# A stored instruction order replaced by another one: same operations, other PSUM banks, other casting engines

## Chip, core and metric

One core of one Trainium2 chip runs the kernel. The metric is the device time of one execution in microseconds (us), from the first to the last thing that the device does for it; the span in a profile runs from the first to the last instruction and is a few us shorter. The core has five engines that each work through a queue of their own in order: TensorE (PE in the profile; its weight loads are the row PEld), VectorE (DVE), ScalarE (ACT), GpSimd (POOL) and SyncE (SP), which here does nothing but issue transfers. Matrix products land in PSUM, eight banks of 128 partitions x 512 float32; VectorE or ScalarE must read them out before a bank can be used again.

## The reference

Two independent layers on bf16 inputs, 2048 tokens by 640 channels each, side by side in the output.

```python
# A: short causal filter of k, product with v, long causal convolution, gate
k_shift = sum over t of k_pad[:, t:t + S, :] * shift_k[:, ks - 1 - t]     # ks = 4
kv = k_shift * v
y = irfft(rfft(kv, 2S) * rfft(ssm_k, 2S))[:S] + kv * ssm_D
a = q * y
# B: 32 heads of 20, 4 segments of 512 tokens, a running memory M, z
for s in range(4):
    p = softmax(qs @ ks.T * scale + causal_mask)
    a_dot = p @ vs
    a_mem = (phi(qs) @ M) / (phi(qs) @ z + 1e-6)
    outs.append(g * a_mem + (1 - g) * a_dot)          # g = sigmoid(beta)
    M, z = M + phi(ks).T @ vs, z + phi(ks).sum(0)
b = concat(outs) @ wo
return concat([a, b], axis=-1)
```

## The kernel before

The program is first recorded and then issued. Python code calls the engines through a `Recorder`; each call, or each run of matmuls into one PSUM group, becomes one of 1505 operations, and each PSUM region that an operation fills becomes one of 471 groups. Nothing is sent to the chip until the end, when `rec.issue(order, base)` goes through the list `order` and issues the operations in that sequence; `base` says at which of the eight PSUM banks each group starts. Both lists are stored in the file as compressed text, `ORDER` and `BASE`. Every engine executes its own operations in the order in which they stand in `ORDER`, and waits only where an operation needs a result, or a buffer or bank that is still being read. All records have one line of the profile, L261, so operations are told apart by the tiles they read and write.

A third string, `EVICT`, has one digit for each of 227 casts that empty a PSUM bank into bf16: 1 puts the cast on VectorE, 0 on ScalarE (`evict`).

The operations, with the short names used below:

- `warm.n`: ten products of zeros at the start. `taps`: the four-tap filter, loaded as `load.skr` (tile `qabs`), turned by TensorE and cast to `taps`. `skd.d`: twenty small ScalarE products that build diagonal matrices of the taps for the five channel blocks d; those of d = 3, 4 read `pack`, a 117.5 KB table of constants loaded as `load.pack` by the GpSimd queue; the others read `ident`.
- Layer A, for each of five blocks d of 128 channels: `A.d.kt` or `ss` (the long filter, turned into tile `kT`), `FK` (its spectrum: eight groups of products with `Wf`, each cast into tile `F`), `BK` (butterflies on VectorE into `Kh`), `ks` (the short filter as products of `kr` with `skd`, multiplied by v on VectorE into `vt`), `FX` and `BX` (the same spectrum of `vt`), `P1` to `P3` and `YB` (complex product and butterflies on VectorE), `I` (inverse, multiplied by q on VectorE).
- Layer B, for eight units u (segment u // 2, half of the heads u % 2): `xt` (x turned into `xT`), `P.u.t` (k and q of token tile t, two groups, cast to `KQ`), `V.u.t` (v, cast to `Va`), `KT` (transposing DMA to `KQT`), `phi`, `kam`, `bound` and `rows` (a bound of each row's logits, written back by four DMAs), `mem` (the memory), `S.u.g.D`, `.A`, `.J` (logits of a head group; each is two ScalarE exponentials of 128x1024 into tile `ET`), `O` (products with v and with the memory), `N` (division on VectorE), and per segment `ot` and `W` (output projection; the last segment's comes at the very end).

The lists interleave the convolution blocks with the attention units, so that the exponentials of ScalarE and the butterflies of VectorE run at the same time, with TensorE feeding both.

```python
def evict(self, out, in_, grp):
    ...
    if EVICT[e] == "1":
        self.nc.vector.tensor_copy(out=out, in_=in_, grp=grp)
    else:
        self.nc.scalar.copy(out=out, in_=in_, grp=grp)
...
order, base = unpack(ORDER, len(rec.ops)), unpack(BASE, len(rec.groups))
with tc.manual_schedule():
    rec.issue(order, base)
```

Of the kernel before, what the change touches and what calls it, by code (L numbers as in the profile page):

```python
# [995 lines left out]
ORDER = r"""
c-jrtgMttW5Czb=Gk0=rwrjI(+um&3wry{=YqM?Jwr#$5zT#w+Y?57aNKVNmxh0R}l_(NXTtrGs6^SI}q@v`L>Jn9=NgOF7p(MXlmGV+nk_aWQR+7{bAQdE|RFeV{Sqe%KEhI&?uv8XEKCPs6rKXsuRMxIiTWU#W
Ni5MNro@oa8cWJ(eyt%v(p?H@LP;gXw2qY3G*Vw`YC~x*^`x9;k=D{uifcCs(gxB<+DZ!vEw!|<l$177TboKh=^^bTtyIx;Qc-(J9c?9bwU0EBdfH6VOM5A$9i^(ql_FAH3Tl6;p*^Lr_LjcVLCWhO=_CWBn8cG|
l3cpT2<a@brG(Vi1d>RGNJA|u4K%C_mN7C=hRY~PDPd%s43)7mTB>OyEupJ*yo{6yQb>b!gErRcx<}S%d?~3-wTaHry|PjlX$tA4$t076lL|UfR%vscB$H)|?2`~(tW#yPY?AI;N@mDL-7l?lnrzbPazK`751p$s
rL`{AHabt6X<PlJEwsHJm6qB;=W9EiC0pg7bkd&MOBZNIJtlp1wj7qux=jwrHr=jAq__6bwc16y>Kxgj+hv^|my6O*Pe`!r)M2_=FUeI|p$m1m_SY>sK(EPMiDM&lr^K~gx>YaBX_+VEb-rAYcy>mX%Pxs(6Lp|2  # L1000
kli{#<J%57FN1WCuGif%Mx$A38>fq8uP&6NwnZ+;GTo<R^{gzG!MaSA>p3~5`!%Jdv7tIdPs&n>k5rb-qT6vjpp$f(PS;a1QV(i)nXEDFzKqsUn%Ex7bD5$`WQNYv>oQeu$qKn4H|4e**2j{>?#L{CDR<?NX0{`m
!B)#reIT<n0UpU~c_nM)jjWVJc2QqQR768Uq_DTLN)jQXWwQ11L@wz&$zoUZvOblha!sE}R@)$JB{9-lcDt&lb)CGIVV1)_N-`uzY&)w@bhw?-50V5S@>DlUPCKE`^ppl7DRS8-IjK`@gq_o=Hqr)KbX?FBh#<H1
yymvg5(9ZHrp2<<_#$bM#|GIqiHSS<Q19wjNrUV9NMqr#-q4$x4!884=CeMCjkkJVze|35pg&~1^|v^9r|<QZCbzU!!0yQ}iHiZ26|XhWe##roh<JFeza^bzLT3Dx43f>p+8>!<FSMY&)C86dAM}g<laKmU$5=uO
g-@CVpS7fY(}_0DfYO#8-!(J@KeUu(fFV03SxV$U8B2wqTGkZPtgscbB38+!8&S?8ps4jjWgBJ1tcp1zA}2;$aVuf7E!YNIE_A{Wt7>5|%Vt;}6h}3yZecOgCR+*Au-qt$APa|@79Qm-5{hAt<;7g9VEIrUg;5rz
QPE0bp1ri%))xVoZ-G+BDxe(dS`jR?0jOuStPB=eJ1d3yRuBQ~U_&iG8rV8pZ0)VJ^+!WnZ(t!Tu`rCxwicUhOxeOJVyO*8SjJ%#4na$+gk`qeMxd2d!3vAYMm7kQF%-iv5-V+i4Mt;YYE8`eTZf}6R#`QWG1=V4
U>us+Sj6H6tAUL+9^n`n9j%jvXJ-qs1YB)vY^`;%C@@RNuJ%{E8LczA+g9sg|Fox7M=$Gb+pLd?ZMXRB&P42Mn=A<va|$+FKXZ#j*cR)CP!@xCFqFG3G?TI)doTinFpSB$$EKn`yJG_O+78=i1+d?0;(-0piHOKR
*2Y1L#va&ZJFN@i@{mPmEhOU^i^qHDz&^Z-!`2gZ(3L58&d%B;>&trR#*`d|RJ>xBZ5q<B7mnHt)W<P9V#n=-rDjLY#7V1*(Ku!2tv9Bl0WMlZYY68gq-AKkV4>I*H!K~S;-=lQ!3?nG7{c2Y+3uKHW8AgLxM%Hn
)goDYUbFjXg!IhJ>z0uN*pv5dEHiOAnxGj@+hWYZ1AAnT?THQIQ=5%B2xFr-kip2pUR;9VoQs9%#0;E=wFqmYxdJ1&2wC~edb2Yh+Ip<R7`8)pF2xf(w`^R7hse!w+<<3zfc6;Ayd24ie2Ud*fjnG^HCTm7e2yG!
gPhF8`MANB$j1c;L4HnV7q-F_w#6k}Mr%x^djW>>f}GAG6feZ0gim8(7Go6Kh#7og#aW4=eI{REGfJ>BH=zpuvLv^lBevotI-mx__&5Gz5P$GHtFk74avQ4gJxg-}w__H|uq?~*Bdhb3T|q6DVtIbx96rJhd}19|
U@))ZG3K&1>vA?Dcmp<MBhF(*?!+}T<~O`S6E<aie!(vMVLgVk>-dhhXvRg{jfNi4!`oMUwi{^97Hr8@T+Hykg!8!vk-Rl;;<bITM*h*%7jgk3`&Yh#`7N~JC+x#gwq<*#f3nwjhbSK8x3Qe-xEB#@89R7XU(cGp  # L1010
9~&6L6?~7+*vMn}fK{yJoA?o{xsnI4mSH`bH}i0Q5NmiGwLQAOvwdvt@9hWnv%VkTQT)Ua1b7VJ%q`r?ZQRZV9@7uwAY=I<9O7ZN^&Q;FuNK=|czoZ@Jv@QE{DseK=dN-5H;(Wx{@@D(^dwsPQ6A$dgwns3*#F_p
{}GDkyLcM^40?)@HHp8qq#oDLK((uzez4O#i{tF#)Dt|zvka>z+0D-}wAS-5dY(NziiX#4n!qD!R6U2D9zoCJ7ZZ6Tji$-`0u%ZV>*W{O*?%*-CikBf=$CkzSD3<6`EN_<S9y(ptc~aQ>x`+ry^mi+L2v3Yw6Ul5
0^ZNRSsG90!t|cOGkR=|rD^@UHSs*2*ZX=t&*c5Rm1p(=UdV5<h+n`XX7y~I-Q#Kw&*FtWr^nG>*4m5uV?N+*=JMiR!i)Js-r^v?!%{xPOM4kF>*YM2j`Nb9+XwmtkFR%G-k-375BBl?ibMS#6KW;D&(}<#!@aUs
@$O#HhxrJv>Q7n66KN8y<|BQSKjUamtj}53$9Q$`=t;GcPxRC})?aXnPxVRulGA*;FZap*hRJk>ukac^(--<m-|ve(xz6@rpW}1=Ef4q-Po=Ybk*CzXo>7;28lC6!eV?!O6q-|)`38T-OuF7fe4{V$O&+MZbd_)R
b-u+9`XNuN>2$T{(af4&*Z5Z7=2>;S@9=E8(|7r9&!C5Wk00@io<(!(ZNKD4J-Z(B9D2s@_+7u}_x-G&^YebeFZ&h0>eu|b-|(A$%a8jBKk29ZwEqW|<?eI
"""
BASE = r"""
c-mc30kQ=l2qH7P|Bb%^HT(YTw3QJeIRFd<sz+jRy?dN_c64=g_q;oTp3i@FZ1$>p9(|HVZ-8vexIrYy61*|F0uj5v$#^nzP{qkt%qZ3%W{_Dok{Dq(H71#r0akn%z}00Jclvx$gQ@^)TGSeh?zfxH6-23;AWyw`
GIDlB{xWvhS!ov&h=r?#|M|G__KO;hF6kM(S=4$QIhkND<bo948P26xGGo5nVNc4hxwzjS4d5wUc|FGXSBGkq=gZwN=<DsC!5i{ii1N6e#&bEJpTGK5VbBdR*N<D$R8}UvVRi9&tDtL19a6U4NyYE>db(@z-nc&e
zj<yB_0_Fy+ZU-_pF7vVd_53;{d!F5fS_B_eBS8~RvQK@  # L1020
"""


# [69 lines left out]
```

## Time and profile before

| | |
|---|---|
| time, three runs | 268.57, 269.68, 269.82 us; median 269.68 |
| profiled execution, span | 266.3 us |
| its own time beside the span | not recorded apart; the median run is 3.4 us over the span |
| PE busy | 257.8 us (97%), 4323 matmuls |
| ACT busy | 248.8 us (93%), 392 instructions |
| DVE busy | 247.1 us (93%), 387 instructions |
| POOL busy | 7.6 us, 20 instructions |
| DMA | 41.84 MB, mean 157 GB/s |
| granted TensorE clock | 1.000 |

An instruction's recorded duration holds a tail that overlaps the next one, so busy time is a little more than the time that the engine gives to the instruction; the chain of work that ended last shows the distance from start to start.

### The profile page before, as it was taken

What the parts mean: (1) busy time and instruction counts of PE and PEld (TensorE: products, weight loads), DVE (VectorE), ACT (ScalarE), POOL (GpSimd) and SP (SyncE); (2) the same over time, 40 slices, a digit from 0 to 9 for tenths busy, and PEclk for the clock granted to TensorE, in tenths of its full rate; (3) what the DMA queues carried; (4) which work ended last, traced back from release to release, by engine and by line L of the source; (5) the groups of instructions that cost most, each with busy time, mean ns of one, the idle gap of its engine ahead of it and who ended that gap; (6) DMA issues with size and microseconds to landing.
All of it is one profiled execution on the core that took longest, in us unless ns stands there. A gap on an engine that the chain in (4) does not pass through costs nothing.

```text
span 266.3 us, 10034 instructions
## 1 busy us (share of the span) xinstructions
PE 257.8 (97%) x4323; PEld 193.0 (72%) x4323; DVE 247.1 (93%) x387; ACT 248.8 (93%) x392; POOL 7.6 (3%) x20
## 2 busy tenths in 40 slices
PE   7999999999999999999999999999999999988994
PEld 3788678778777778877767777778776876665871
DVE  0599999999999999999999999999999999999971
ACT  2878999999999999999999999999999999999953
POOL 8300000000000000000000000000000000000000
PEclk9999999999999999999999999999999999999999
DMA  7999898999989797996999699958990099345034
GB/s 217 292 214 218 197 180 187 126 233 205 172 200 175 142 180 162 173 154 126 154 173 201 164 185 182 211 107 113 181 186 3 29 158 149 87 108 128 28 66 116
DMA packets 126604, 41.84 MB, mean 157 GB/s; under 512 B 114107, under 2 KB 125376, under 8 KB 126432
## 3 DMA queue, kind: packets, MB, share of 16 engines
q1 hardware_dynamic: 126416, 41.07, 80.1%
q8 instruction: 34, 0.56, 0.9%
q0 software_dynamic: 144, 0.13, 0.1%
q14 instruction: 10, 0.08, 0.1%
HBM read 11.96 MB, written 5.24 MB: 65 GB/s over the span
## 4 chain that ended last, share of the span: by engine, by line
PE 62%; ACT 28%; DVE 5%; issue 2%; DMA 1%; POOL 0%; DVEq 0%; ACTq 0%; POOLq 0%
PE ps L261 62%; ACT ET L261 19%; ACT F L261 3%; ACT KQ L261 1%; ACT PP L261 1%; DMA qabs<-in_A_shift_k_dram 1%; ACT Va L261 1%; DVE vt L261 1%; ACT outb L261 1%; DVE Y L261 1%; DVE Kh L261 1%; ACT qabs L261 1%; DVE pq L261 0%; ACT xT L261 0%; DVE o L261 0%
## 5 line engine op out<-in xcount | busy, mean ns | idle before, releaser
L261 ACT ACTIVATE ET<-ps 128x1024 bf16<-128x1024 f32 x160 | 162.6, 1122 | 0.4 <-PE ps L261 0.2
L261 PEld LDWEIGHTS <-xT 128*128 128x128 bf16 x640 | 57.3, 98 | 27.8 <-issue 6.8
L261 PE MATMUL ps<-wqkv,xT 128*128 128x320 bf16 x480 | 77.0, 299 | 0.4
L261 ACT CAST F<-ps 128x512 bf16<-128x512 f32 x72 | 43.3, 686 | 0.9 <-DVE F L261 0.8
L261 PE MATMUL ps<-Va,ET 128*128 128x21 bf16 x1280 | 41.8, 173 | 0.0
L261 PEld LDWEIGHTS <-ET 128*128 128x128 bf16 x1280 | 39.1, 96 | 2.1 <-issue 1.0
L261 PE MATMUL ps<-KQT 32*128 32x128 bf16 (+3 forms) x896 | 35.7, 239 | 0.3
L261 PEld LDWEIGHTS <-Wf 128*128 128x128 bf16 x320 | 29.8, 98 | 6.1 <-issue 1.3
L261 ACT CAST KQ<-ps 128x320 bf16<-128x320 f32 x54 | 25.5, 513 | 2.4 <-PE ps L261 2.3
L261 PE MATMUL ps<-wo,xT 128*128 128x320 bf16 (+2 forms) x160 | 25.5, 299 | 1.3 <-ACT ET L261 1.3
L261 PEld LDWEIGHTS <-KQT 32*128 32x128 bf16 (+1 forms) x896 | 16.1, 92 | 9.9 <-issue 8.2
L261 PE MATMUL ps<-kT,Wf 128*128 128x256 bf16 x160 | 21.8, 273 | 0.1
L261 PE MATMUL ps<-vt,Wf 128*128 128x256 bf16 x160 | 21.2, 273 | 0.0
L261 PE MATMUL ps<-Y,Wi 128*128 128x256 bf16 x160 | 20.8, 273 | 0.0
L261 DVE TENSOR_TENSOR o<-ps,rr 128x640 bf16<-128x640 f32 x24 | 19.7, 819 | 0.4
L261 DVE TENSOR_TENSOR Y<-Y,pq 128x2048 bf16<-128x2048 bf16 (+1 forms) x20 | 18.6, 937 | 0.0
L261 PE MATMUL ps<-Mbd,PqT 128*128 128x84 bf16 x96 | 18.3, 203 | 0.1
L261 DVE TENSOR_TENSOR pq<-Xh,Kh 128x2048 bf16<-128x2048 bf16 x15 | 18.2, 1215 | 0.0
L261 PE MATMUL ps<-skd,kr 128*128 128x128 bf16 (+4 forms) x124 | 17.9, 270 | 0.0
L261 PEld LDWEIGHTS <-kr 128*128 128x128 bf16 x124 | 15.6, 147 | 2.5 <-issue 0.8
L261 PEld LDWEIGHTS <-Wi 128*128 128x128 bf16 x160 | 14.8, 98 | 2.5 <-issue 0.6
L261 ACT ACTIVATE PP<-KQ 128x1280 bf16<-128x1280 bf16 x12 | 15.9, 1361 | 0.0
(87 smaller groups left out, 355.6 us busy)
## 6 DMA issues: line engine op xcount, KB each, us to landing
vt<-in_A_v_dram SPq DMA_DIRECT2D x10, 256.0 KB
pq<-in_A_q_dram SPq DMA_DIRECT2D x10, 256.0 KB
kT<-kT SPq DMA_DIRECT2D x32, 64.0 KB
out_dram<-pq SPq DMA_DIRECT2D x8, 256.0 KB
out_dram<-outb SPq DMA_DIRECT2D x12, 160.0 KB
Wf<-c_wf SPq DMA_DIRECT2D x4, 256.0 KB
Wi<-c_wi SPq DMA_DIRECT2D x1, 1024.0 KB
kb<-kr SPq DMA_DIRECT2D x4, 256.0 KB
```

What stands on the lines that cost most here:

```text
L261: f(*[fix(a) for a in args], **{k: fix(v) for k, v in kw.items()})
```

## The change

The code of every operation stays. Three stored texts are replaced: `EVICT`, `ORDER` and `BASE`. They come from a search over a model of the kernel which, new, charges half the TensorE clock for stretches where TensorE streams little.

```diff
-EVICT = ("10100001110000001000000010000000...
-         "000000000101000100100100000000000000010000001100001000000000000000000000010110010000100")
+EVICT = ("01111100100001110010000010000000...
+         "000000000010000110100100001000010010000000000000111000000100001000100100000101000000000")
...
 ORDER = r"""
-c-jrtgMttW5Czb=Gk0=rwrjI(+um&3wry{=YqM?Jwr#$5zT#w+Y?57aNKVNmxh0R}l_(NXTtrGs6^SI}q@v`L>Jn9=NgOF7p(MXlmGV+nk_aWQR+7{bAQdE|RFeV{Sqe%KEhI&?uv8XEKCPs6rKXsuRMxIiTWU#W
...
+c-jTQ17HvU6a>(_kF;zr+qP}DY}>YN+t#veEZes2_kak<ifqV^9LR}W$c;S6i+revDoBl}sETNahiXWOh^T~eh>HR!gwk*%KxL#y3=~9pWJZ1zL1C0Z1yqvKQbekwD54`KN+1o&qOwFmGAPPOag;<|1fe$KBQdg|
...
 BASE = r"""
-c-mc30kQ=l2qH7P|Bb%^HT(YTw3QJeIRFd<sz+jRy?dN_c64=g_q;oTp3i@FZ1$>p9(|HVZ-8vexIrYy61*|F0uj5v$#^nzP{qkt%qZ3%W{_Dok{Dq(H71#r0akn%z}00Jclvx$gQ@^)TGSeh?zfxH6-23;AWyw`
...
+c-mEyi@L)g2!oNE@BhZrpLllGe(R`05+ZHeb}zR&KR;1fTd=ZEw9b1G-)Jl6X59B6^X~O|-nCmZSAco{+Y*)p-A<OD)y=z+f9pya3)a+H!0n*lJ3(!!ZS5C#@)jUo&W2@r3bLE3K(R?p!d7&U>S@E1ASP9VI8G(;
...
```

Unpacked and set against the list of operations, the new texts say this. The 1505 operations are a permutation of the same ones; an operation moves by 14 places on average and 550 at most. 392 of 471 groups start at another bank. 49 casts change engine:

| cast (elements a partition) | DVE before | DVE after | ACT before | ACT after |
|---|---|---|---|---|
| F (512) | 8 | 8 | 72 | 72 |
| KQ (320) | 10 | 10 | 54 | 54 |
| Va (320) | 1 | 6 | 31 | 26 |
| outb (320) | 8 | 6 | 16 | 18 |
| xT of segment 0 (640) | 1 | 4 | 3 | 0 |
| xT of the last segment (512) | 1 | 1 | 4 | 4 |
| PP, last W (512) | 1 | 0 | 3 | 4 |
| qabs (512) | 1 | 0 | 7 | 8 |
| kT (512) | 2 | 2 | 2 | 2 |
| taps (40) | 1 | 0 | 0 | 1 |

By place, ACT between its first and its last exponential has KQ 46 -> 44, Va 27 -> 23, outb 16 -> 18, xT 2 -> 1, qabs 6 -> 7, F 59 -> 61, and 64-wide skd products 2 -> 0. DVE between its first `BX` and the `N` of the third head group of unit 7 has KQ 5 -> 7, Va 1 -> 5, outb 8 -> 6, xT 0 -> 1, F 5 -> 3, qabs 1 -> 0, and one 16-wide product less.

The first operations of each queue (before | after):

```
POOL  load.pack, load.skr, load.bt, zero KQ, zero Drow, zero kr, load.Drow, zero Mbd, zero qabs, zero KQ, zero Mbd, 2 copies pack->KQ, zero PP ...
    | load.skr, zero KQ, load.bt, zero PP, zero Mbd, zero KQ, load.pack, zero Mbd, zero Drow, load.Drow, zero kr, zero qabs, 2 copies pack->KQ ...
SP    w.0.0, ident, x0, x3, x1, x2, sk, w.0.1, Wf 3 0 2 1, k (transposing), v, v, w.0.2, KT.0 2 1 3 0 ...
    | ident, x2, x3, x1, x0, w.0.0, sk, Wf 2 1 3 0, w.0.1, k (transposing), w.0.2, v, v, KT.0 0 2 1 3 ...
PE    warm x9, taps, xt.0, warm, xt.3, xt.1, P.0.0, xt.2, beta, P.0.1, P.0.3, kt 3 1 2, P.0.2, P.0.0, kt.0, P.0.1, P.0.2, FK x8, ks, ks, P.0.3, ks, ks, kam.0, V.0.0, V.0.2, FX x8 ...
    | warm x9, taps, xt.3, xt.2, beta, xt.1, warm, xt.0, P.0.3, P.0.2, P.0.1, kt 3 1 2 0, P.0.0, FK.2 x2, FK x5, P.0.1, FK, P.0.0, P.0.3, P.0.2, ks x4, kam.0, V.0.0, FX x8 ...
ACT   skd.1, xt.0, skd.3, xt.3, beta, beta, xt.2, P.0.0, kt.1, skd.3, skd.0 x4, kt.0, skd.2, P.0.1, phi, FK ...
    | taps, skd 1 2 1, beta, skd 2 0, beta, Va, skd 0 0, Va, skd.4, Va, skd 2 3 4, Va, skd 0 4 3 4, kt.2, kt.1, P.0.0, skd.2, phi, FK ...
DVE   zeros, taps, xt.1, P.0.1, beta, P.0.3, P.0.2, P.0.0, kt.2, phi, kt.3, P.0.2, FK.0 ...
    | zeros, xt.3, xt.2, beta, beta, xt.1, xt.0, P.0.3, P.0.2, Mbd, Mbd, P.0.1, kt.3, kt.0, phi, FK.2 ...
```

"load.bt" is the 32 numbers beta; "Va" in the ACT row is a 64-element write of a constant column; "w.h.i" is the weight of half h (0: k, 1: q, 2: v), 400 KB each; each x is 160 KB, sk 512 KB, each Wf 256 KB, k 512 KB, each v 256 KB.

At the end, the TensorE order after the last `S` of unit 7 is ot.3.2, A.4.I.0, O.7.3.0, A.4.I.2, O.7.3.1 to 3, ot.3.3 before, and A.4.I.2, A.4.I.0, ot.3.2, O.7.3.0 to 3, ot.3.3 after; then the same sixteen pieces of `W.3` and ot.3.4 in another sequence. The cast of ot.3.0 goes from ACT to DVE, those of ot.3.2 and W.3.2 from DVE to ACT.

More of the change, by code (lines that the diff above doesn't have):

```diff
@@ L1000 @@
[L1000 to L1012, printed above, removed]
@@ new lines @@
+6ly>a36Wt)iK0RjLoDQ#<Vb{iNP#+NiCU<MP{=1ik`bxU98D337N{w$(HPCp23=7f4bT>~q_)(NViFn+(GE?}2(8c_-H~6aNLeW$b)_5npaY6a9Hc`hl#{B`5B<>#JrEmxQBMj=Z}h|fBtcpXLt&{Xr6ehaU?}R#
+K#amTjKLrjlHnMEjwml(&_Ft4G^)vX)R3?kjD}J|Mq(@`U?L`C5~g4(8p%=#gT_)_mdRc;m3=5FYb01I$YR+nYo&=Sk&UuRx=A=}!8Gj00nCx<=po%@2IfjDX)Vp9jkJ)1Xf6w6p=`!VX)80)QdY?^w3A;l3ms&&
+%#-%gNp?s_IgV{|2=nC#W}~n4l*8yOz2qo*%LdsleWa@_l6BHW=3p+aVy9e2Ke>i^*nx{Uf!*jY>*WfD$pE>80G!83?2;`qTrOZf2Fh;Pi8B}^BP5QFm#tWUb2y8wvPTwTJ0{8m*(*^sn#R+8GDh|w1j}Wd#MRUq
+Ur%8d7GWD!$VwcL#Ym!KC5`Tvq`Dl(Wd%-Suq?$v87c`FU6)~qq|_yNjuVnf6LO>+lIwVgqjE$>$t|qH4cx?GNu;YWT4HEoeTqkzB$MTs+{QGSE;HmlGUx-u=M=ev$B4!Zm@3bZQKNFEJi$u@>OH*13uMw)m?dv8
@@ new lines @@
+Ti#*~F3JYHLki8T@pwtH=zFZiWl67r%&LiaMK&T9v+Fusm5<1w>v0!3^_rZKbCQ&2Wtb-86B(hyHMV}jQ+X!Ic~VB|2TajZGF4AY3MS@f#N-!5XA*`;E{&<V^}K9CMyBNj$;5#gOCL%)re<8`)$4LYZpt^@mSB8E
+Y{p?8?ZfYQB)8;_+?9KBUmi;uX465MPv6Q9#NY$TuRk$f-^)AcuLCrh_GNgyl3$ph**Q&<>l-PcY4x>C*XNQ>Gqa$+lzvR0WA%l6kS|h5v#_v!m5=fpSvgMs;4l6GOsJnE8*{LvewNZ&N>lQikl*EpI45c<{uHIK
+j1JXFnx3IqM2%&&sAga&R?_e+rxDnRqqMSC(VQ%%qqT&F;T)Z;gEbe6>kN&^s#;C+aEONGOpV0Znw#ady3W;#T0;x7rjF4HT9kQNoSj*W<(ZGA8IH5G1cUUY&evKRz<FAh6<AvrXdSJq^|Zb&(lYGNa%`ZB^|!Rs
+A}q=E+FlE?6eHOHcF_E6t%cZ7Ghu^9Hrf)c$fdeW2eOTZvC52XZM7@I+6s+hVlA`>D{;AYVPr<JR@zdla0G|2J6CE{Yox2R8+&sQM{*b!>QD~mY8}qT+ElBtiN>^bT9sqiT-9P(GmXNHx>m=s7i-Y0qi)hp+F66O
@@ new lines @@
+i+0s;7GP_%Cli?J6n4`dT7Xk&+Fi#nq4m^lI-WZ;zV*^T+pfK}kM`B>_E)NNvnH|_me__`O-8gHwpIVhB@VNG*56#ALENHAj2cR7bC2HPUfr(;G_?JZgPP3x={}vndkk+8tQHSxa=Xl(I+1-WnjO{@wo8xbQN7DL
+jBC3!rS-Mwc2?tA2TNsXtgD6SISs9sv@W~ZF+Hvw?Sx*@lX_WG+bB-sDXquzI+~)VwK?6U^P+~b8Jx)rn$#w-KG$(FBWN>5)U=k)Zs={jqj&X;KHx2F$OgQpH?<KXX*-Lo?Jd1s)$4jq@9P6?!pzo~gRLna>MRbi
+u{OZMXjomsjP^*g*khf|ha6=~IfqX)gFV%`9B9vUK9_Mhhua8S!IhlHO!izyTTffW1zgWAwwRr)m#yL$8)pl7pIL3Zb+#vL#|>P~Y_^6`v^}%iNSkQ6ZIJc0jl5xN`IJ}rjCm}tJ!cE%u$(r@S~8d2WE<Y*WZT4i
+R=`>@zfG~WY)$u2UeJnIVJm9Ithi0J={CV`a5Fm+{z9kObr!N2MxSXVESQz7ij}k%e96CdjiG%DZ?UqKvRM|!YuGpYXFsf_bzqQHwQc-v)vdHuvoiMH%GyW!VCAfqZRIE1!JjtQ>ezNZVr`pe<*kA>u!i=SjcmS!
@@ L1016 @@
+!@Qc`x2IOotNSRg<D-3~KeNQr(VtsgPa{cWjHi}PUc)E)SfAoAY^qQ5=|0&f`3hg<NoA$a@R^=WW_c=kV=wKkE%GIPzz_OjpY3yeuFvzOzRy$2GGFc)Wxg-){l3mO_<GMN3q6x;^i3Y@n>~f(l6SV+lgk!g<6Awe
+q?JRy%`;0n$s=n$i)54SzQcF=Vc+GueUI<;Bc4HW$Th$1XZ@JxmJ^;`(#ugl>Bs$!-}UQ$%J2C(zwf90jNkAOzv<`wmS6CTe#tNU6~F5L0kc@{bN
 """
 BASE = r"""
[L1018 to L1019 removed]
@@ L1020 @@
-zj<yB_0_Fy+ZU-_pF7vVd_53;{d!F5fS_B_eBS8~RvQK@
+c-mEyi@L)g2!oNE@BhZrpLllGe(R`05+ZHeb}zR&KR;1fTd=ZEw9b1G-)Jl6X59B6^X~O|-nCmZSAco{+Y*)p-A<OD)y=z+f9pya3)a+H!0n*lJ3(!!ZS5C#@)jUo&W2@r3bLE3K(R?p!d7&U>S@E1ASP9VI8G(;
+(oUUdfuEo{N{qb_<770-iVhR*k~^<1gl)nL`ZV-39&YLjuT5SKqvKmk*JCzmF&vt`ueM~(#p5tET3VHZ>#CZwO)^YV(nO1uh0?8)OF1~R73yhD<ncVLRHvbH2^?FTi!*sC#FiJ$b4z7wjzYc9`6QUG{iVtx4!Pz!
+)p2)bHF0ZZ<LPuwb!#@Bk5B*Ck@u~<E}x42)A{T1%w_(Y+nJg1V!o~-;{zqV1^x
 """
```

13 lines of the change are left out of this document (6 added, 7 removed).

## The prediction

> **What bounds the kernel now.** I read the page first: three engines over 93% busy, and a chain that changes hands between them.
>
> ```profile
> span 266.3 us, 10034 instructions
> PE 257.8 (97%) x4323; PEld 193.0 (72%) x4323; DVE 247.1 (93%) x387; ACT 248.8 (93%) x392; POOL 7.6 (3%) x20
> PEclk9999999999999999999999999999999999999999
> PE 62%; ACT 28%; DVE 5%; issue 2%; DMA 1%; POOL 0%; DVEq 0%; ACTq 0%; POOLq 0%
> ```
>
> Then a table of busy time in stretches that I cut at the head, the middle and the end (columns: stretch, its length, busy time of PE, PEld, DVE, ACT, POOL with the number of instructions, granted clock, DMA share, GB/s).
>
> ```profile
> 0.00:4.30 4.30, 3.04 (x8) 1.12 (x9) 0.33 (x1) 0.00 (x0) 3.05 (x12) 1.00 0.53 154
> 4.30:7.45 3.15, 2.34 (x31) 1.52 (x30) 0.31 (x2) 2.32 (x4) 3.15 (x7) 1.00 1.03 344
> 7.45:30.00 22.55, 22.55 (x196) 18.21 (x197) 19.59 (x34) 18.02 (x47) 1.39 (x3) 1.00 1.04 237
> 30.00:130.00 100.00, 99.69 (x1695) 76.33 (x1693) 99.30 (x147) 99.86 (x155) 0.00 (x0) 1.00 0.93 172
> 130.00:250.00 120.00, 117.51 (x2195) 86.73 (x2192) 119.30 (x191) 119.90 (x178) 0.00 (x0) 1.00 0.75 136
> 250.00:263.00 13.00, 12.71 (x209) 9.13 (x207) 8.29 (x16) 8.38 (x13) 0.00 (x0) 1.00 0.28 65
> ```
>
> The reader should see three stages. From 30 to 250 us ScalarE stands idle for 0.24 us and VectorE for 1.4 us: they are both the bound, and that stage lasts as long as the work that the lists give them. Before 30 us and after 250 us they have holes (4.5 and 3.0 us of 22.55 in the head) while PE has none: there PE's order decides. The chain of waits says the same, with PE alone at both ends.
>
> ```profile
> 1.22 0.70 POOL pack L261
> 1.92 3.56 DMA qabs<-in_A_shift_k_dram
> 7.45 44.03 PE ps L261 x556
> 54.34 0.32 ACT Va L261
> 67.28 0.48 ACT F L261
> 121.94 0.40 DVE KQ L261
> 212.24 2.03 ACT ET L261 x2
> 242.90 1.72 ACT ET L261 x2
> 249.25 13.48 PE ps L261 x216
> ```
>
> The first rows are a start-up chain: GpSimd issues the load of `pack` ahead of the tap filter, and PE waits for the latter. The single rows are prices from start to start: a 320-wide cast takes 0.32 us on ScalarE and 0.40 on VectorE, a 512-wide one 0.48 on ScalarE.
>
> **What the new lists could gain by the clock: nothing.** The search charges half clock where TensorE streams little, but every slice of the row PEclk is 9 and every stretch has 1.00. Half speed is seen in the zero products of the start alone, whose mean is 558 ns against 379 for products of the same size later (the first stretch's 1.00 doesn't show it).
>
> ```profile
> L261 PE MATMUL ps<-o 128*128 128x512 bf16 x10 | 4.0, 558 | 1.3 <-DVE o L261 1.3
> L261 PE MATMUL ps<-wo,xT 128*128 128x512 bf16 x20 | 5.0, 379 | 0.0
> 5.52 0.62 PE L261 MATMUL ps<-ident,qabs 5*64 5x5 bf16 x12 [0.67 <-DMA qabs<-in_A_shift_k_dram]
> ```
>
> PE's longest wait is the 0.67 us of the last row, and it kept full clock through it. Both lists start with nine such products. Term: 0. The Trainium skill (TensorE: Matmul & The Clock Gate, The HAM clock gate) has the clock fall to half after an idle window of about 3.4 us. This trace, with 0.67 us at most and no fall, doesn't contradict it, and by that rule too there is no stretch to win back.
>
> **The head, step by step.** Rows from the timeline (start, duration, instruction, idle time before) and the list of transfers (KB, us from issue to landing):
>
> ```profile
> 2.93 0.39 POOL L261 MEMSET KQ<- 128x64 bf16 x1
> 3.72 0.51 POOL L261 DMA_DIRECT2D Drow<-in_A_ssm_D_dram  x1 [0.24 <-POOL kr L261]
> 4.22 0.40 POOL L261 MEMSET Mbd<- 128x336 bf16 x1
> 7.03 1.38 POOL L261 MEMSET PP<- 128x1536 bf16 x1
> pack<-c_pack POOLq DMA_DIRECT2D x1, 117.5 KB, 3.5
> Drow<-in_A_ssm_D_dram POOLq DMA_DIRECT2D x1, 1.2 KB, 4.6
> 6.18 0.20 DVE L261 COPY taps<-ps 128x40 f32<-128x40 f32 x1 [4.98 <-PE ps L261]
> 6.42 0.40 ACT L261 ACTIVATE skd<-ident,taps 128x128 bf16<-128x128 bf16 x1 [0.63 <-DVE taps L261]
> 7.34 0.82 DVE L261 CAST xT<-ps 128x640 bf16<-128x640 f32 x1 [0.96 <-PE ps L261]
> 8.63 1.53 PE L261 MATMUL ps<-wqkv,xT 128*128 128x320 bf16 x10
> 10.00 0.89 PE L261 MATMUL ps<-ident,kT 128*128 128x128 bf16 x12
> 11.17 0.35 ACT L261 ACTIVATE skd<-pack,taps 128x64 bf16<-128x64 bf16 x1
> 11.42 1.27 ACT L261 ACTIVATE skd<-ident,taps 128x128 bf16<-128x128 bf16 x4
> 12.59 0.57 ACT L261 CAST kT<-ps 128x512 bf16<-128x512 f32 x1
> 13.69 0.27 PE L261 MATMUL ps<-kT,Wf 128*128 128x256 bf16 x1
> 17.30 0.38 PE L261 MATMUL ps<-skd,kr 128*128 128x512 bf16 x1
> 27.77 1.23 DVE L261 TENSOR_TENSOR Xh<-F 128x2048 bf16<-128x2048 bf16 x1
> ```
>
> First, the tap filter's load comes first on GpSimd, at 1.22 instead of 1.92, and lands 0.70 earlier. PE is free 0.67 before it started, so `taps` starts at 4.85: gain 0.67.
>
> Second, three of the four 640-wide casts of x go from ScalarE to VectorE, which stood idle there (4.98 and 0.96 in the rows). One takes about 0.75 (0.82 less the overlap). The two small beta steps between them wait for ScalarE, so the third starts near 7.8, and the third projection group waits for its end at 8.55, 0.3 late. That replaces the wait for a cast that P.0.0 has now: 0.
>
> Third, ScalarE now makes 15 of the diagonal products, and six small beta pieces, before it casts kt.2, the piece that the first spectrum needs. From 5.51 (taps, again 0.66 after PE's start) the products start at 5.75. Nine of 128 columns at 0.29 (1.17 for four, 11.42 to 12.59), six of 64 at 0.25 (11.17 to 11.42) and 0.7 for the small pieces, some 0.25 of that a wait for VectorE, make 5.1: kt.2 would be cast from 10.85, and with 0.6 for the cast the first FK starts at 11.45. Before, FK starts at 13.69 with three projection groups more behind it; at 0.68 each (8.63 to 10.00 for two) equal work is 11.65. So -0.2, if `pack` is there.
>
> Fourth, `pack` was the first load of GpSimd and is now behind the tap load, beta, and memsets: 1.22 + 0.53 + 0.39 + 0.52 + 1.38 + 0.40 + 0.39 = 4.83 (the issues of the two loads are about as long as Drow's 0.51). The first product that reads it comes up at about 8.45. Landing is bounded by 3.5 after the issue (pack itself, with an empty machine: 8.33, no wait) and 4.6 (Drow, issued at 3.72 among the loads: 9.43, a wait of 1.0). I take 4.6, whose time of issue is nearest. FK then starts at 12.45, 0.8 later than equal work. The other end stays at -0.2. The Trainium skill (DMA: Bandwidth & Descriptors, Anatomy of one DMA — SWDGE (gpsimd) path) fits about 2.0 us plus bytes over 436 GB/s: an estimate of 2.3 us for pack, which would land at 7.1 and give the -0.2. The rows, 3.5 and 4.6, disagree with it.
>
> The SP queue: ident and x now go ahead of the first weights, Wf ahead of w.0.1, w.0.2 ahead of v. By 7.45 about 1.75 MB have moved (154 and 344 GB/s in the first two stretches), then 237 KB each us. Wf.2 is the 1840th KB, there near 8, needed at 12.45. w.0.1 is the 3008th, there at 12.8, needed behind seven of eight FK groups (3.6 for all, 13.69 to 17.30), at 15.6. v comes 400 KB later, at 18.8 rather than 17.1; its first use, on VectorE, is behind the eight groups (3.6), four projections (2.7) and a ks group, so after 18.8: a thin cover, and if it is gone, v's lateness goes to VectorE, 1.7 at most. The transposing load of k keeps its place. Term 0.
>
> **The middle.** ScalarE, between its first and last exponential, gets four 320-wide casts fewer (KQ -2, Va -4, outb +2), two 512-wide ones more (xT -1, qabs +1, F +2) and two small products fewer: -4 x 0.32 + 2 x 0.48 - 2 x 0.25 = -0.8. VectorE, from BX to the last normalisations, gets four 320-wide more (KQ +2, Va +4, outb -2), two 512-wide fewer (xT +1, F -2, qabs -1; 0.60 each, the 0.48 of ScalarE plus the same quarter) and a tiny one fewer: +1.6 - 1.2 - 0.1 = +0.3. ScalarE starts the stage with PE, 0.8 late, and ends it at 0.0. VectorE's start is BX, at 27.77: 14.1 after the first FK. Now two projection groups more stand between the two on PE, 1.4, so it comes 15.5 after FK, at 27.9: +0.1, and the stage ends at +0.4. Both engines feed on PSUM banks that the other one empties, so the later counts: +0.4. The other 450 or so moved operations are the same work in another sequence and cost nothing if the sequence has no holes; that is the bet, and its price is below.
>
> **The end.** PE runs 13.48 us without a pause from 249.25. After ot.3.3 the same pieces follow; ahead of it A.4.I.2 moves before O.7.3.0, which leaves PE nothing to do while it waits for the last exponential, but removes as much after it. The cast of W.3.2 leaves VectorE, which has 4.7 us free in the last stretch. The last cast and the store stay: 0.
>
> **Sum.** 0 (clock) + 0.4 (head and middle, on VectorE) + 0 (end) on the span of 266.3: 266.7. The median run, 269.68, is 3.4 above that span; I put the sum on it: 270.1.
>
> **Rivals.**
> - *Faster: the middle gets denser, and pack lands early.* With pack after 3.5 us ScalarE's stage ends at -1.0 and VectorE's, with BX 1.0 earlier, at -0.6. A pair of exponentials takes 1.72 in one row and 2.03 in another; three pairs in tighter places give 0.9. Sum -1.5: 268.2. For it speaks the 3.5 row; against it that the middle has 1.6 us of idle time in all to lose.
> - *Slower: holes in the middle.* 392 groups change banks. If a new neighbour holds a bank a little longer, PE feeds an exponential late, and as both engines are full the time is not made up.
>
> ```profile
> PE ps L261 <- ACT ET L261: 1.9, 5, 0.5
> ```
>
> A hole of that size, 0.5, in each of four segments, is +2.0, with the +0.4: 272.1. It decides from two holes on. Against it: the old list, of the same kind, has 0.24 us of idle ScalarE in 220.
> - *Slower: pack lands later than 10.4.* Each us beyond 9.43 is a us for ScalarE, and through the first FK for PE and VectorE; from 1.0 us on it is over 0.5%: 271.4 with 1.3.
> - *The clock does fall* in the new list, at a place where PE has less to do. A 512-wide product loses 0.18 by the two rows above; ten in one spell cost 1.8: 271.9. The granted clock speaks against it.
>
> **Chances and range.** A run of this kernel tells 0.5%, 1.35 us, from no change; 268.57 to 269.82 is the spread of the three. Forecast, within 0.5%: 0.50. Faster rival 0.22. Holes 0.15, late pack 0.10, clock 0.03: slower 0.28. The range reaches from just under the faster rival, 267.9, to the holes, 272.1, and leaves out some 0.2, denser middles and more holes than priced. The forecast's own range, by the two ends of pack's landing, -0.6 and +0.4, and three tenths for v's thin cover, is 269.1 to 270.4.
>
> **What would show it.** In the changed profile: PE's wait of 0.67 gone and VectorE's first cast near 5.9; ScalarE waiting about 1 us for `pack` around 8.5 (none: the fourth step is wrong); the first FK near 12.5; ScalarE and VectorE over 99% busy from 30 to 250 (under that: holes); PEclk 9 throughout; the last cast near 263. The forecast is wrong if the middle shows waits of ScalarE for PE, or if PE's head costs or gains more than 1.5 us.

## The result, and the profile after

The changed kernel takes 272.41 us (median of six runs, 271.72 to 272.98) against 268.54 for the kernel before in the same comparison: 1.0131 times as long, 95% interval 1.01 to 1.0161. It is slower by 1.3%. The forecast was 270.1 and no change; the measured time is 0.3 over the upper end of the range. The miss is larger than that: the forecast stood on 269.68, the median of the first three runs, so it was a change of +0.4, and the upper end +2.4, against +3.9 by these medians (3.5 by the ratio). The profiled run took 271.87 with a span of 270.1, 3.8 over the span before. (Medians are over all runs, ratios over the undisturbed ones.)

The page of the changed kernel:

```profile
span 270.1 us, 10048 instructions
PE 256.8 (95%) x4323; PEld 192.8 (71%) x4323; DVE 250.8 (93%) x390; ACT 248.4 (92%) x389; POOL 7.2 (3%) x20
PEclk9999999999999999999999999999999999999999
PE 51%; ACT 32%; DMA 6%; issue 5%; SPq 2%; DVE 2%; POOL 1%; ACTq 0%; DVEq 0%; POOLq 0%
```

DMA holds 6% of the chain, where it had 1%. The same stretches as before (length; busy PE, PEld, DVE, ACT, POOL; clock; DMA share; GB/s):

```profile
4.30:7.45 3.15, 2.63 (x32) 1.65 (x31) 1.20 (x2) 1.55 (x7) 2.10 (x7) 1.00 0.95 274
7.45:30.00 22.55, 20.53 (x181) 16.70 (x179) 20.75 (x37) 15.08 (x40) 1.81 (x4) 1.00 0.97 232
30.00:130.00 100.00, 98.67 (x1639) 75.05 (x1637) 98.41 (x143) 97.46 (x150) 0.00 (x0) 1.00 1.02 178
130.00:250.00 120.00, 116.02 (x2178) 86.28 (x2175) 118.84 (x190) 119.85 (x177) 0.00 (x0) 1.00 0.76 134
```

In the head TensorE now has 2.0 us of holes where it had none, and ScalarE 7.5 against 4.5. From 130 us on ScalarE is as full as before. The chain of waits names the places (start, us, what):

```profile
1.24 0.64 POOL qabs L261
2.47 1.39 POOL PP L261
4.19 6.79 DMA pack<-c_pack
13.42 0.48 ACT kT L261
13.94 18.53 PE ps L261 x153
...
89.81 0.58 SPq L261
90.49 5.59 DMA KQT<-qabs
96.12 22.46 PE ps L261 x393
```

A load on GpSimd opens it, and a second transfer, KQT at 90.49, stands in the middle of what was to be the full stage. The head in the timeline, and the first and the last exponential:

```profile
4.19 0.57 POOL L261 DMA_DIRECT2D pack<-c_pack  x1
5.21 0.62 PE L261 MATMUL ps<-ident,qabs 5*64 5x5 bf16 x12
7.13 0.44 PE L261 MATMUL ps<-ident,Y 128*128 128x128 bf16 x5 [0.52 <-DVE xT L261]
8.15 2.20 PE L261 MATMUL ps<-wqkv,xT 128*128 128x320 bf16 x15
11.01 0.35 ACT L261 ACTIVATE skd<-pack,taps 128x64 bf16<-128x64 bf16 x1 [1.87 <-DMA pack<-c_pack]
13.33 1.04 ACT L261 CAST kT<-ps 128x512 bf16<-128x512 f32 x2
13.94 2.45 PE L261 MATMUL ps<-kT,Wf 128*128 128x256 bf16 x21 [1.94 <-ACT kT L261]
35.33 1.94 ACT L261 ACTIVATE ET<-ps 128x1024 bf16<-128x1024 f32 x2
257.38 1.94 ACT L261 ACTIVATE ET<-ps 128x1024 bf16<-128x1024 f32 x2 [0.45 <-PE ps L261]
```

The same two exponentials in the kernel before:

```profile
32.51 1.02 ACT L261 ACTIVATE ET<-ps 128x1024 bf16<-128x1024 f32 x1
253.54 1.94 ACT L261 ACTIVATE ET<-ps 128x1024 bf16<-128x1024 f32 x2 [0.19 <-PE ps L261]
```

So the loss divides at two rows. The first exponential is 2.82 us later (35.33 - 32.51), the way from the first to the last is 1.02 longer (222.05 against 221.03), and the end gives 0.1 back: 3.75. Both engines that bound the middle stay over 97% busy, so a late start is not made up there. The list of waits adds (us in total, times, longest):

```profile
PE ps L261 <- ACT ET L261: 3.9, 13, 0.5
PE ps L261 <- ACT kT L261: 1.9, 1, 1.9
PE ps L261 <- DMA KQT<-qabs: 0.5, 1, 0.5
```

Before, the first of these was 1.9 in 5 times and the other two were not there.

### The profile page after: what moved, and what is told of

Its sections match the earlier page's. It is cut to its first block, busy times and chain, and to the rows that moved or that the text cites. A ratio compares the mean times of both kernels' runs of the same rounds, so it can differ in the third digit from the quotient of the medians.

```text
span 270.1 us, 10048 instructions
## 1 busy us (share of the span) xinstructions
PE 256.8 (95%) x4323; PEld 192.8 (71%) x4323; DVE 250.8 (93%) x390; ACT 248.4 (92%) x389; POOL 7.2 (3%) x20
## 4 chain that ended last, share of the span: by engine, by line
PE 51%; ACT 32%; DMA 6%; issue 5%; SPq 2%; DVE 2%; POOL 1%; ACTq 0%; DVEq 0%; POOLq 0%
PE ps L261 51%; ACT ET L261 18%; ACT F L261 4%; ACT KQ L261 3%; DMA pack<-c_pack 3%; SPq L261 2%; DMA KQT<-qabs 2%; ACT PP L261 2%; ACT outb L261 1%; DMA pq<-in_A_q_dram 1%; ACT Va L261 1%; POOL PP L261 1%; ACT skd L261 1%; ACT qabs L261 0%; DVE Xh L261 0%
## 5 line engine op out<-in xcount | busy, mean ns | idle before, releaser
L261 PEld LDWEIGHTS <-xT 128*128 128x128 bf16 x640 | 58.8, 97 | 28.6 <-issue 7.6
L261 PEld LDWEIGHTS <-Wf 128*128 128x128 bf16 x320 | 29.1, 97 | 8.7 <-issue 4.4
L261 PE MATMUL ps<-KQT 32*128 32x128 bf16 (+3 forms) x896 | 32.9, 239 | 0.6 <-DMA KQT<-qabs 0.5
L261 PE MATMUL ps<-vt,Wf 128*128 128x256 bf16 x160 | 22.1, 273 | 0.3 <-ACT ET L261 0.3
L261 PEld LDWEIGHTS <-KQT 32*128 32x128 bf16 (+1 forms) x896 | 15.0, 92 | 9.0 <-issue 7.6
L261 ACT ACTIVATE PP<-KQ 128x1280 bf16<-128x1280 bf16 x12 | 16.5, 1371 | 0.0
```

The costliest lines, as they stand in the source:

```text
L261: f(*[fix(a) for a in args], **{k: fix(v) for k, v in kw.items()})
```

## The experiments

First theory (A): the head's loss is `pack`, landing late ahead of a ScalarE list that holds the cast of kt.2 behind it. Rival (B): the new middle sets the end whatever the head does. All twelve, each compared with the kernel before on its own chip:

| run | what | median us | ratio to before, 95% interval | first to last exponential, us |
|---|---|---|---|---|
| before | | 268.54 | 1 | 221.03 |
| changed | | 272.41 | 1.0131 (1.01 to 1.0161) | 222.05 |
| pack_early | changed, pack second on GpSimd | 270.43 | 1.0084 (1.0045 to 1.0123) | 221.66 |
| casts_first | changed, six skd behind the casts | 271.62 | 1.0105 (1.008 to 1.0129) | 221.41 |
| both | the two together | 271.99 | 1.0119 (1.0094 to 1.0145) | 221.89 |
| pack_third | changed, pack third | 271.14 | 1.0092 (1.0058 to 1.0126) | 224.65 |
| old_head | old 220 operations, new rest | 270.92 | 1.0099 (1.0063 to 1.0135) | 223.09 |
| old_head_long | old 283 operations, new rest | 271.03 | 1.0077 (1.0048 to 1.0107) | not read |
| new_head | new 220 operations, old rest | 272.28 | 1.0135 (1.01 to 1.0171) | 223.80 |
| old_skr_first | before, tap load first | 268.68 | 1.0009 (0.9987 to 1.0031) | 221.28 |
| old_x_first | before, tap load first, x ahead of weights | 269.27 | 1.004 (1.0014 to 1.0067) | 221.03 |
| wo_late | changed, wo behind rows.2 | 273.17 | 1.0185 (1.0159 to 1.0212) | 222.87 |
| mended | changed, five repairs | 272.22 | 1.0147 (1.0115 to 1.0179) | 223.25 |
| head_mended | changed, four repairs of the head | 272.44 | 1.015 (1.0103 to 1.0197) | 222.28 |

The last column is the difference of two rows like those quoted above, from one profile each.

**pack_early.**

```diff
+pack, skr = [next(o.idx for o in rec.ops if o.key == ("load", n)) for n in ("pack", "skr")]
+order.remove(pack)
+order.insert(order.index(skr) + 1, pack)
```

> The changed kernel with the load of pack issued second on GpSimd, right behind the tap filter's, instead of seventh. Theory A (the late table): the two GpSimd loads in the traces so far were served after all that SyncE had issued before them; at 1.9 us that is little, so pack lands before 6 us, ScalarE's wait of 1.87 us for it is gone, kt.2 is cast near 11.5, the first FK starts near 12.0 instead of 13.94, and everything behind comes some 1.9 us earlier: 270.5 us (270.2 to 270.8) against 272.4 for the changed kernel. Theory B (the middle): the wait goes as well, but the time stays within 0.5 us of 272.4, because the middle of the new list sets the end. Theory C (bandwidth): the 117.5 KB come ahead of x and cost it 0.4 to 0.8 us at 154 to 274 GB/s, so the transposed x is late by that much and the time is 271.0 to 271.4.

Measured 270.43, the value of A. Its timeline:

```profile
1.86 0.59 POOL L261 DMA_DIRECT2D pack<-c_pack  x1
11.90 1.03 ACT L261 CAST kT<-ps 128x512 bf16<-128x512 f32 x2
12.51 2.45 PE L261 MATMUL ps<-kT,Wf 128*128 128x256 bf16 x21
33.90 1.94 ACT L261 ACTIVATE ET<-ps 128x1024 bf16<-128x1024 f32 x2
```

The wait for pack is gone, the first FK and the first exponential come 1.43 us earlier (13.94 and 35.33 before), the span is 1.8 shorter (268.3 against 270.1). By the ratios it is 0.5%, 1.3 us, with intervals that overlap; both have the same sign. It is a third to a half of the loss. The first exponential is still 1.39 behind the kernel before, and C's late x did not show: the first projection started at 8.02 against 8.15.

**casts_first.** The same wait taken away from its other end.

```diff
+late = [i for i in order if rec.ops[i].key in (("skd", 3), ("skd", 4))][:6]
+order = [i for i in order if i not in late]
+kt1 = next(o.idx for o in rec.ops if o.key == ("A", 0, "kt", 1) and o.eng == "ACT")
+at = order.index(kt1) + 1
+order[at:at] = late
```

> The changed kernel with pack still late, but with the six skd products that read pack moved on ScalarE behind the casts of kt.2 and kt.1. Theory A (ScalarE stood queued behind the table while TensorE waited for kt.2): kt.2 is cast when TensorE has made it, near 11.0, the first FK starts near 11.9, TensorE's wait of 1.94 us is gone; ScalarE gets through its head list 0.9 to 1.2 us earlier. The time falls by 0.9 (ScalarE's gain) to 1.9 (TensorE's): 270.5 to 271.5 us. Theory B (the middle): 271.9 to 272.9, as the changed kernel. If the gain is near 1.9, TensorE's start carried the loss; near 0.9, ScalarE's backlog did.

Measured 271.62, just over the range of A, the span 268.5. kt.2 is cast without waiting for pack, and the wait turns up on VectorE, whose beta step reads pack too and stands ahead of the cast of kt.3:

```profile
11.12 1.07 ACT L261 CAST kT<-ps 128x512 bf16<-128x512 f32 x2 [1.15 <-PE ps L261]
13.14 2.02 PE L261 MATMUL ps<-kT,Wf 128*128 128x256 bf16 x17 [0.71 <-DVE kT L261]
```

So in the changed kernel three engines stood behind the late table (ScalarE 1.87 us, VectorE 0.82, GpSimd 4.35), and moving one of them aside only uncovers the next.

**pack_third.**

```diff
-order.insert(order.index(skr) + 1, pack)
+order.insert(order.index(bt) + 1, pack)
```

> The changed kernel with the load of pack third on GpSimd, behind the tap filter's and beta's, issued near 2.5 us. Theory F (a GpSimd load is served when the bytes that SyncE had issued before it have moved): by 2.5 SyncE has issued ident and three of x, 512 KB, which have moved by 4.2 us; pack's packets begin at 3.9 to 4.4 and it lands at 5.3 to 6.2, 2.8 to 3.7 us after its issue. Rival G (a GpSimd load among other traffic takes a fixed 4.6 us or more, as the nearest row of before had it): it lands at 7.1 or later. Rival H (6.8 us, as in the changed kernel, whatever the place): 9.3. ScalarE needs it at 9.1, so by F and G the time is that of pack second, 270.0 to 270.6 us; by H 270.2 to 270.8.

The list of transfers and the wait that made this run long:

```profile
pack<-c_pack POOLq DMA_DIRECT2D x1, 117.5 KB, 3.7
```

```profile
PE ps L261 <- DMA KQT<-qabs: 1.3, 1, 1.3
```

Issued at 2.47, pack landed 3.7 us later: F holds, G and H fall. The median, 271.14, is 0.5 over what F gave, and why is not shown. In the profiled run, the longest of the six (273.16), TensorE waited 1.3 us for KQT in the middle: the hole of the changed kernel again, longer, with nothing changed near it.

**old_head, new_head, old_head_long.** The lists spliced: one list's first operations, then the other's remaining ones in its order.

```diff
+order_h, base_h = unpack(ORDER_HEAD, len(rec.ops)), unpack(BASE_HEAD, len(rec.groups))
+head = set(order_h[:220])
+order = order_h[:220] + [i for i in order if i not in head]
+base = [base_h[g.idx] if any(o.idx in head for o in g.ops) else base[g.idx] for g in rec.groups]
```

> The first 220 operations in the old order with the old banks and casting engines (up to the first exponentials), all the rest in the new order. Theory A (the head holds most of the loss: the first exponential is 2.82 us later in the changed kernel, of 3.75 us at the end): 269.4 to 269.8 us, that is 268.5 plus the 0.9 to 1.3 that the new middle adds. Theory B (the new middle costs it, and a better head only waits there): 271.5 to 272.4.

> The first 220 operations in the new order with the new banks and casting engines, all the rest in the old order. Theory A (the head): 271.1 to 271.6 us, that is 268.5 plus 2.6 to 3.1. Theory B (the middle): 268.5 to 269.5, because a middle without holes of its own would swallow the late start.

> The first 283 operations in the old order with the old banks and casting engines (to about 48 us), all the rest in the new order. The first splice, at 220 operations, lost 1.24 us between 35 and 42 us, beside 0.3 to 0.8 later. Theory A (that loss belongs to the joint; behind 50 us the new middle costs 0.2 to 0.6): 268.8 to 269.5 us, unless this joint costs too, which the waits of TensorE near 48 us would show. Theory B (the new middle needs longer whatever stands ahead of it): 270.5 to 271.

None came out as A had it: old_head (270.92) lies between the ranges of A and B, new_head (272.28) above both, old_head_long (271.03) at the end of B's. With the old head the first exponential is at 32.77, only 0.26 late, and the new rest then needs 223.09 us, 2.06 more than the old one. With the new head it is at 35.08 and the old rest needs 223.80. The two losses add up to 2.3% where the change has 1.3%, so the joints cost something by themselves: in old_head the first exponential is 2.56 us ahead of the changed kernel's, and the PP step that starts at 43.83 there starts here at 42.61, only 1.22 ahead. The long splice (1.0077; in its profile the clock falls to half for 3.41 us from 98.23, so its middle is not read) did not get rid of it. What the splices do show: a good head in front of the new rest is not enough, so B has a part in it; they do not say how much. TensorE's waits for exponentials go with the rest of the list: 4.4 us in 14 times in old_head, 2.4 in 6 in new_head.

**both.** The edits of pack_early and casts_first together.

> The two edits together: pack issued second on GpSimd, and the six skd products that read it behind the casts of kt.2 and kt.1. With pack early alone ScalarE still casts kt.2 only at 11.90 us, because the products, the beta pieces and a wait of 1.0 us for VectorE's beta step stand ahead of it; with the casts first alone VectorE stood 0.8 us behind pack. Theory A (what is left in the head is ScalarE's list ahead of kt.2): kt.2 cast at 11.0, first FK near 11.9 instead of 12.5, time 0.5 to 0.7 us under pack early alone: 269.7 to 269.9 us. Theory B (what is left is TensorE's: its two waits of 0.52 and 0.33 us for VectorE's casts of x, and the order of its groups): no more than 0.2 us under pack early alone, 270.2 to 270.5.

271.99 is against A and B alike. The profile shows something that those of pack_early and casts_first, with the same products in the same order, do not:

```profile
5.76 1.25 PE L261 MATMUL ps<-ident,Y 128*128 128x128 bf16 x10
8.84 3.03 PE L261 MATMUL ps<-wqkv,xT 128*128 128x320 bf16 x15
```

In the changed kernel the fifteen products took 2.20, and ten transposes 0.73 (at 5.76): here TensorE ran slowly until past 9 us and the first FK started at 13.35. Nor did the second edit help by itself: TensorE waited 0.97 at 16.2 for a cast of F on VectorE, and VectorE had waited 1.89 for a cast on ScalarE that the six products now stand ahead of. Inconclusive for the theories.

**old_skr_first, old_x_first.** Two parts of the change alone, in the old list: the order of the loads at the start.

```diff
+behind(find("load", "skr"), order[order.index(find("load", "pack")[0]) - 1])
+last = max((find("xn", t)[0] for t in range(4)), key=order.index)
+behind(find("load", "w", 0, 0), last)      # old_x_first alone
```

> The kernel before with one edit: the load of the tap filter is issued ahead of that of pack on GpSimd. Theory A: TensorE's wait of 0.67 us before the taps goes (0.3 to 0.67 us, as far as the products of zeros run at half speed until then and x has landed), and since TensorE has no idle time from 7.45 to 219 us the gain reaches the end: 267.9 to 268.2 us. Rival: x or the first weights land no earlier, so the wait moves to the transposes of x: 268.4 to 268.6, no change.

> The kernel before with the tap filter's load ahead of pack's on GpSimd and, on SyncE, ident and the four of x ahead of the first weights (as in the new list). With the tap load alone TensorE's wait moved to x (0.45 and 0.46 us), because 400 KB of weights were served ahead of it. Theory A: both waits go, the first projection starts at 6.8 to 7.1 us instead of 7.45, unless the weights, which then land behind x, are late for it (1072 KB had moved by 6.1 to 6.5 us, and a load's end is seen some 0.7 us later: 6.8 to 7.2); the gain reaches the end: 268.0 to 268.3 us against 268.5. Rival: the wait moves on to the weights, 268.5 to 268.8.

The first changed nothing in the time (268.68, ratio 1.0009) and moved the wait for the tap filter to x, as its rival had it:

```profile
6.28 0.45 PE L261 MATMUL ps<-ident,Y 128*128 128x128 bf16 x5 [0.45 <-DMA Y<-in_B_x_dram]
7.69 0.45 PE L261 MATMUL ps<-ident,Y 128*128 128x128 bf16 x5 [0.46 <-DMA Y<-in_B_x_dram]
```

The second moved it on to the first weights:

```profile
8.47 0.84 PE L261 MATMUL ps<-wqkv,xT 128*128 128x320 bf16 x5 [2.05 <-DMA wqkv<-in_B_wk_dram]
```

Its first projection starts 1.02 us later than in the kernel before (7.45), the first exponential 1.00 later, the last one 1.00 later, and the median is 0.4% up. So the order ident, x, weights, which the new list has, costs the head about 1 us: 400 KB of weights behind 672 KB of ident and x are late for the first projection. In the changed kernel no wait for these weights is seen: its first projection starts at 8.15, right behind the transposes of x, which other waits hold up.

**wo_late.** After pack_third I looked for what makes KQT late: in the new list the 800 KB of `wo` are issued right ahead of the four small rows.2 transfers (89.81 and 90.49 in the chain above); in the old list `wo` goes at 75.5.

```diff
+behind(find("load", "wo"), find("rows", 2)[-1])
```

> The changed kernel with one load moved in SyncE's queue: the 800 KB of wo go behind the four small rows.2 transfers instead of right ahead of them (89.8 and 90.5 us in its trace); nothing needs wo before 127 us. Theory D (a hole in the new middle comes from there): if transfers are served in the order of issue, 800 KB at about 200 GB/s hold rows.2 back by 4 us; without them TensorE's wait of 0.51 us for KQT at 95.6 goes, with ScalarE's of 0.41 and VectorE's of 0.36 behind it, and runs in which these waits were longer (1.3 us in the kernel with pack third) gain more: 271.4 to 272.0 us against 272.4. Rival E (rows.2 is late because bound.2 stands behind VectorE's wait for a store): the wait stays, 272.2 to 272.6.

Slower, 273.17. The KQT wait at 96 is gone, as D has it, but the 4 us that it took from `rows.2` are now taken from the load of q that follows, and the product with q waits:

```profile
94.83 0.45 SPq L261 DMA_DIRECT2D wo<-in_B_wo_dram  x1
96.78 2.89 SPq L261 DMA_DIRECT2D pq<-in_A_q_dram  x2
104.97 0.69 DVE L261 TENSOR_TENSOR pq<-ps,pq 128x512 bf16<-128x512 f32 x1 [1.44 <-ACT ET L261]
105.71 1.03 PE L261 MATMUL ps<-Y,Wi 128*128 128x256 bf16 x8 [0.75 <-DVE pq L261]
```

The releaser named for VectorE, an exponential, had ended; what the step reads beside PSUM is q. The packets of the trace agree: wo's 640 packets of 1280 bytes pass at 91.8 to 94.8 in the changed kernel with those of rows.2 right behind, and at 95.9 to 99.3 here. On balance the exchange costs little (the ScalarE pieces that lie between 78.2 and 126.0 us in the changed kernel take 0.33 longer here), so the 0.8 in the median is not explained by it. The profiled run, 274.4, had one more loss, which is told at the end.

**mended, head_mended.** All repairs, and those of the head alone.

```diff
+behind(find("load", "pack"), find("load", "skr")[0])
+early = [i for i in order[:80] if rec.ops[i].key in (("skd", 3), ("skd", 4))]
+behind(early, find("skd", 3)[-1])
+for g, bank in ((1, 1), (5, 4), (4, 6)):
+    base[g] = bank
+behind(find("load", "wo"), find("rows", 2)[-1])                          # mended alone
+behind([A], order[order.index(find("A", 1, "P1")[0]) - 1])               # mended alone; A is VectorE's bound.2 step
+order.insert(0, order.pop(order.index(find("load", "w", 0, 0)[0])))      # head_mended alone
```

> The changed kernel with five repairs, one for each place where its traces lost time: pack issued second on GpSimd; all six early skd products that read pack moved into the 4.3 us in which ScalarE waits for FX; three start-up groups on other banks so that the third transpose of x need not wait 0.52 us for the first one's cast; wo behind rows.2; VectorE's bound.2 step ahead of the step that waits for a store. Theory A (the loss is these places): first projection at 7.5 us, kt.2 cast at 10.5, first FK at 11.3, first exponential 2.3 to 2.8 us earlier than in the changed kernel, no wait for KQT at 95: 268.7 to 269.3 us, that is the time before and up to 0.7 more. Theory B (the new middle itself is slower: TensorE waits 13 times for exponentials, 3.9 us in all, against 5 times and 1.9 us before): 269.7 to 270.6, no better than pack early alone.

> The changed kernel with four repairs of its head and nothing else: pack issued second on GpSimd; the six early skd products that read it in ScalarE's 4.3 us hole before FX; the three start-up groups on other banks; and, new, the first weights back at the front of SyncE's queue, as in the old list (the kernel with all repairs waited 0.65 us for them at 7.7, and the old list with x ahead of them 2.05 us). Theory A (the head's loss is pack, the weights behind x, and the bank wait): first projection at 7.5 to 7.7 us, first FK near 11.3, first exponential 32.5 to 32.8 us after the start against 35.33 in the changed kernel; from there ScalarE has 0.74 us less work than in the old list but 1.1 to 1.8 us more stalls in every run of the new middle so far, so the time is 0.4 to 1.1 us over the kernel before. Theory B (the new middle takes back what its head gains, as with the old head in front of it, which ended 2.3 us behind the kernel before): 2.0 us or more over the kernel before, no better than pack early alone.

Both fell short of A by 2 us and more, and mended lies above the range of B as well. By the ratios (1.0147 and 1.015 against 1.0131) neither is faster than the changed kernel, though their profiled runs are (spans of 269.5 and 269.3 against 270.1). mended had its first exponential at 33.50, 1.83 earlier than the changed kernel; TensorE waited 0.65 for the first weights at 7.74 (the order of old_x_first) and 0.68 for other weights at 36.4, and the moved `wo` cost it the same wait for q as in wo_late, 1.63 on VectorE at 100.3. head_mended had none of these, but TensorE was slow again until past 9 us:

```profile
6.01 1.25 PE L261 MATMUL ps<-ident,Y 128*128 128x128 bf16 x10 [0.18 <-DMA Y<-in_B_x_dram]
8.83 2.59 PE L261 MATMUL ps<-wqkv,xT 128*128 128x320 bf16 x15
```

Its first exponential is at 34.29 instead of the 32.5 to 32.8 of A. Its runs lie between 271.2 and 275.3, and four of the six had a mean granted clock of 0.992 to 0.994 where all six of the changed kernel had 0.998 or more; so by number it speaks for B, but what the head's repairs are worth on their own it does not settle. No version here beats the kernel before.

## Why the prediction was wrong, step by step

**Right.** The clock brought nothing: PEclk is 9 throughout and every stretch has 1.00. PE's wait of 0.67 for the taps is gone (it was the longest behind PE's first product; the 1.3 of the zeros row lies ahead of it). ScalarE waits for pack, in the place named. The end gave 0.1 against 0.

**The taps, +0.67.** They start at 5.21, not 4.85: gain 0.31. The nine products of zeros, 3.59 us before, took 4.02, because TensorE's speed rose later in this run.

**Fourth step, pack: the term that was mis-sized.** The issue was forecast for 4.83 and came at 4.19, but the landing took 6.8 us from there, not 3.5 to 4.6: 11.0 instead of 9.43. The row of Drow that I took as nearest was near in time, not in what stood ahead of it; nor was pack's own 3.5 that of an empty machine, since 358 KB from SyncE had moved when its first packet ran. The first FK came at 13.94 instead of 12.45. This is the rival "pack lands later than 10.4", and its price, 271.4 for a us or so, was about right: pack_early shows 1.4 at the first exponential. The Trainium skill's fit (DMA: Bandwidth & Descriptors, Anatomy of one DMA — SWDGE (gpsimd) path; an estimate of 2.3 us for pack) is farther off than the rows were; nearest to it, 2.0 for so few bytes, come the tap filter's and beta's loads of the changed kernel, 2.6 and 2.3, with at most 352 KB issued ahead of them.

**Third step, "-0.2".** pack_early has pack there in time, as this step asks, and still casts kt.2 at 11.90 instead of 10.85, with the first FK at 12.51 instead of 11.45. Of the 1.05, 0.75 is VectorE's beta step, for which ScalarE waits 1.00 us instead of 0.25 (rows in the last section). The terms of the step, 2.6, 1.5 and 0.7, also make 4.8 and not 5.1, unless the 0.25 is added to them. And the equal work was more than three projection groups: from the first FK to the first exponential the three profiles with the old list take 18.82 us, the changed kernel, pack_early, pack_third, mended and head_mended 21.39, that is 2.57 more, not 2.04. So an equal first exponential needs the first FK at 11.12, not 11.65. The loss at the first exponential, 2.82, is then 1.43 for the late pack, 0.86 for this step (12.51 against 11.65) and 0.53 for the count of the work.

**The SP queue, "Term 0", and the second step, "0".** I asked of Wf, w.0.1 and v whether they come in time, and not of w.0.0, which the new list puts behind ident and x. old_x_first puts that at 1.0 us by itself; in the new list it shows once other waits are gone (0.65 in mended). The second step, the casts of x on VectorE, was also not 0: the third transpose waits 0.52 for a bank that the first cast holds.

**The middle, "+0.4".** Two things failed. The late start was not made up: 2.82 at the first exponential, 3.75 at the last work. And the middle was not free of holes. Between its first and last exponential ScalarE is busy for 220.71 us in both kernels, and idle for 1.34 instead of 0.32; VectorE is busy for 219.25 and 219.26, and idle for 2.80 instead of 1.77. So the whole 1.02 is idle time, and the 0.8 of work that ScalarE was to save did not shorten it: the casts and products do take 0.98 less from start to start, but the 158 exponentials take 145.84 instead of 144.87 (13 of them over 0.96 us, 7 before), for a reason that no run shows. KQT's 0.51 is seen on ScalarE as one hole of 0.41; the rest lies in gaps under 0.15. That is the rival "holes", priced at 2.0 for four holes of 0.5; I gave it 0.15 beside 0.10 for the late pack and treated the two as alternatives, while both came. That the measured time still lies close to the upper end of the range is luck: that end was priced for the holes alone. Before the prediction the row 30 to 130 showed DMA busy 0.93 of the time; I looked at the transfers of the head alone, and moved transfers were counted as "the same work in another sequence".

**What stays open.** What makes the exponentials longer and the many small gaps; what a repaired head is worth in the time, since the profiles gain by it and the ratios do not; and whether a repaired new list would equal the old one.

## What to carry to other kernels

A moved load is priced by what has been issued ahead of it on other queues too (here on SyncE's), not by the time that the same load took elsewhere: add up the bytes issued before it, and read from the traffic when they will have moved. Look at every consumer of each load that changes place, in the middle too, where DMA is busy most of the time. In a stage where two engines are over 99% busy, nothing makes up for a late start (the 1.00 us of old_x_first reaches the last exponential as 1.00), so the us lost ahead of it are lost for good; and removing one wait ahead of it is worth only the distance to the next one.
